# Two of a fused kernel's orders: an eviction moved from ScalarE to VectorE, and units 4 and 5 of the attention placed behind block 1's halves

## The chip, the cores and the metric

The kernel runs on 1 core of one Trainium2 chip. The metric is the device time of one execution in microseconds. TensorE (PE in the rows) multiplies matrices, VectorE (DVE) and ScalarE (ACT) do the elementwise work, GpSimd (POOL) a few small pieces, and SP issues the transfers. Each engine executes its own instructions strictly in program order and waits on semaphores where it needs another's result.

## The reference, cut to what matters

```python
# attention: B, H, S, D = 4, 8, 576, 64
scores = scale * np.matmul(q, k.transpose(0, 1, 3, 2))
scores = np.where(causal, -1e9, scores)
a = np.exp(scores - scores.max(-1, keepdims=True))
a /= a.sum(-1, keepdims=True) + 1e-09
local = np.matmul(a, v)
mem_out = (phi(q) @ M_prev) / (phi(q) @ z_prev + 1e-06)
attn = g * mem_out + (1 - g) * local
# feed-forward on x of shape (2304, 512), d_ff = 2048
h = x @ w_in
r = np.maximum(h, 0.0)
out = (r * r) @ w_out
```

All inputs and outputs are float32. Each token's 8 x 64 attention values are one row of x.

## The kernel before

**Attention units.** The list `order` holds 24 units, counted here from 0: one pair of heads of one batch entry with some of its four tiles of 128 queries. Units 0 to 3 are batch entry 0 with tiles 1 and 2 ("lo"), units 4 to 7 the same with tiles 3 and 4 ("hi"). A unit computes scores of a tile on TensorE into the PSUM tile `sp` (L583), VectorE evicts them with the mask and the row maximum into `e` (L604, `tensor_tensor_reduce`, two heads), ScalarE takes the exponential (L624), and the weights are transposed. In units 0 to 2 (`full`) that is done in float32 on TensorE: up to four transposed tiles in the PSUM tile `pxa`, evicted to `aF` (L643 to L646) by the engine that `PXE` names, its first letter for the first `pxa` of a tile of queries and its second for the second. Only tile 2 has a second one: two of 128x128. From unit 3 on the weights are split into two float16 halves `a`, by ScalarE (L662) and VectorE (L664), and SP transposes them by DMA to `aT` (L668). TensorE multiplies with the values into `acc` (L688), and VectorE adds to `feat`, the unit's features (L691). Unit i's buffers for k, q and v (`kd`, `qm`, `vv`) are loaded ahead as the unit two or three before gives them up.

**Blocks of tokens.** Four units of equal tiles make the features of 256 tokens, a block. Block 0 is the first 64 tokens of all four batch entries; block 1 is tiles 1 and 2 of batch entry 0, so units 0 to 3. `token_halves` (L706) makes a block's input: squares for a scale (L715), a high half on ScalarE (L722) and a low half on VectorE (L723), float16, for each of two tiles of tokens, and for each a transpose by DMA into `xT` (L724). `moe` then multiplies with the weights' halves: `up` (L989 to L991), relu and square on ScalarE, halves `gh` and `gl` (L1001, VectorE), and `oacc` (L960 to L962). Block 0 adds its groups of weights into `o` (L978).

**The order.** `ORD` merges the generators: units 0 to 3, then the weights' preparation, and block 0 beside them, then the other units with the blocks' matmuls behind. Within that, the framework's scheduler places each instruction on its engine by its own estimate of when it can start. `later(eng, x)` adds an edge to such an instruction that only orders: `x` is placed behind the instruction that `gate[eng]` holds, and no semaphore is waited for. Before the change such edges hold back weights (`put`) and the first unit (`lead`) behind block 0's tokens.

Of the kernel before, what the change touches and what calls it, by code (L numbers as in the profile page):

```python
# [14 lines left out]
AF = mybir.ActivationFunctionType  # L15
ALU = mybir.AluOpType
# [25 lines left out]
NEF = 3  # L42
NES = 6
PXT = 'av'
PXE = 'aa'
PHI = 1
ZW = D + 1
MW = 576
# [28 lines left out]

FIRST = 4
WA = 0
WE = 8  # L80
WE2 = 16
WH = 11
# [16 lines left out]
def fused_kernel(ctx: ExitStack, tc: tile.TileContext, t0_d, kk_d, qv_d, beta, w_in, w_out, out):  # L99
    nc = tc.nc  # L100
# [65 lines left out]
    gate = {}  # L166
# [286 lines left out]
    def attention(b, p, tiles, ld, after, early, sfull, full, ap, ap_early):  # L453
# [118 lines left out]
        def scores(group):  # L572
            sps = ps.tile([P, 2, 512], F32, tag="s", name="sp")
            c = 0
            at_col = []
            for i, ka, kb in group:
                qc = slice(QT[i][0] - D, sum(QT[i]) - D)
                cs = slice(c, c + kb - ka)
                at_col.append(cs)
                with tc.high_priority():  # L580
                    for x, (qt, kt) in enumerate(terms):
                        for h, hd in enumerate(heads):
                            mm = nc.tensor.matmul(  # L583
                                sps[:, h, cs], qt[hd, qc], kt[hd, ka:kb], start=x == 0, stop=x == len(terms) - 1
                            )
                            if x == h == 0 and lead:
                                later("t", mm)
                            if behind:
                                tc.add_manual_dep(mm.ins, behind.pop().ins.name, AFTER, reason="a batch comes late")
                            while parts:  # L590
                                tc.add_manual_dep(mm.ins, parts.pop().ins.name, WHOLE, reason="a batch starts whole")
                c = cs.stop
            for (i, ka, kb), cs in zip(group, at_col):
                q0 = QT[i][0]
                if ka == 0:
                    row[i] = (
                        ap.tile([P, 2, S], F32, tag="e", name="e", bufs=EB if ap is at else EB2),
                        at.tile([P, 2, 2], F32, tag="mx", name="mx", bufs=4),
                        at.tile([P, 2], F32, tag="sm", name="sm", bufs=4),
                    )  # L600
                e, mx, _ = row[i]
                s = int(ka > 0)
                for h in range(2):
                    nc.vector.tensor_tensor_reduce(  # L604
                        out=e[:, h, ka:kb],
                        in0=sps[:, h, cs],
                        in1=mask[:, 448 - q0 + ka : 448 - q0 + kb],
                        scale=-0.125,
                        scalar=3e38 if s == 0 else mx[:, h, 0:1],
                        op0=ALU.add,  # L610
                        op1=ALU.min,
                        accum_out=mx[:, h, s : s + 1],
                    )

        for i in [t for t in TORD if t in tiles]:
            q0, n = QT[i]
            ke = q0 + n
            for group in SGROUP[i]:
                scores(group)
            ns = 2 if any(ka for g in SGROUP[i] for t, ka, _ in g if t == i) else 1  # L620
            e, mx, sm = row.pop(i)
            for h in range(2):
                bs = mx[:n, h, ns - 1 : ns]
                ex = nc.scalar.activation(  # L624
                    e[:n, h, :ke], e[:n, h, :ke], AF.Exp, bias=bs, scale=-1.0, accum_out=sm[:n, h : h + 1]
                )
            behind[:] = [ex]
            u0, ur = e[:n, :, 0:D], e[:n, :, D:ke]
            if full:
                nb = 1 + i  # L630
                aT = at.tile([P, 8, P], F32, tag="aT16", name="aF")
                cols = [(0, D)] + [(D + c * P, P) for c in range(i)]
                for b0 in range(0, 2 * nb, 4):
                    bn = min(4, 2 * nb - b0)
                    px = ps.tile([P, 4, P], F32, tag=PXT, name="pxa", bufs=2)
                    for x in range(bn):
                        h, c = divmod(b0 + x, nb)
                        c0, cw = cols[c]
                        nc.tensor.transpose(px[:cw, x, :n], e[:n, h, c0 : c0 + cw], ident)
                    lo = [x for x in range(bn) if (b0 + x) % nb == 0]  # L640
                    for x0, xn, pn in [(x, 1, D) for x in lo] + runs([x for x in range(bn) if x not in lo]):
                        dst, src = aT[:pn, b0 + x0 : b0 + x0 + xn, :n], px[:pn, x0 : x0 + xn, :n]
                        if PXE[b0 // 4] == "a":  # L643
                            nc.scalar.copy(dst, src)
                        else:
                            nc.vector.tensor_copy(dst, src)  # L646
            else:
                nb = 1 + 2 * i
                tg = TAGS[i]
                if i < 3 and 3 - i in started:  # L650
                    a, aT, o = (*a12, 6 if i == 2 else 0)
                else:
                    a = ap.tile([P, tg * P], F16, tag=f"a{tg}", name="a")
                    aT = ap.tile([P, tg, P], F16, tag=f"aT{tg}", name="aT")
                    o = 6 if i == 2 else 0
                    if i < 3:
                        a12 = (a, aT)
                started.add(i)
                a, aT = a[:, o * P : (o + 2 * nb) * P], aT[:, o : o + 2 * nb]
                av = a[:n].rearrange("p (h x) -> p h x", h=2)  # L660
                for x, o0, w in ((u0, 0, D), (ur, P, i * P)):
                    nc.scalar.mul(av[:, :, o0 : o0 + w], x, SC)  # L662
                for x, o0, w in ((ur, P, i * P), (u0, 0, D)):
                    nc.vector.scalar_tensor_tensor(  # L664
                        out=av[:, :, o0 + w : o0 + 2 * w], in0=x, scalar=SC, in1=av[:, :, o0 : o0 + w],
                        op0=ALU.mult, op1=ALU.subtract,
                    )
                nc.sync.dma_start_transpose(out=aT[:, :, :n], in_=a[:n])  # L668
            nc.vector.scalar_tensor_tensor(
                out=sm[:n], in0=sm[:n], scalar=1e-9, in1=gm[:n, h0 : h0 + 2] if full else vz[:n],  # L670
                op0=ALU.add, op1=ALU.mult,
            )
            nc.vector.reciprocal(sm[:n], sm[:n])
            yield

            acc = ps.tile([P, 2, D], F32, tag="av", name="acc", bufs=2)
            for h in range(2):
                hd = slice(h * D, (h + 1) * D)
                if full:
                    mms = [(aT[: D if c == 0 else P, h * nb + c], v[: D if c == 0 else P, c, hd]) for c in range(nb)]  # L680
                else:
                    vh, vl = (vs[:, h, :, x * D : (x + 1) * D] for x in range(2))
                    mms = [(aT[:, h * nb], vh[:, 0]), (aT[:, h * nb], vl[:, 0])]
                    for c in range(1, i + 1):
                        hi, low = aT[:, h * nb + c], aT[:, h * nb + i + c]
                        mms += [(low, vh[:, c]), (hi, vh[:, c]), (hi, vl[:, c])]
                for x, (lhs, rhs) in enumerate(mms):
                    nc.tensor.matmul(acc[:n, h], lhs[:, :n], rhs, start=x == 0, stop=x == len(mms) - 1)  # L688
            for h in range(2):
                xo = memx[:n, i - 1, h]  # L690
                x = nc.vector.scalar_tensor_tensor(  # L691
                    out=xo, in0=acc[:n, h], scalar=sm[:n, h : h + 1], in1=xo, op0=ALU.mult, op1=ALU.add
                )
                step.setdefault(me, x)
            yield
# [10 lines left out]
    def token_halves(b, blk, xts, out_scale):  # L706
# [12 lines left out]
        nc.vector.reciprocal(sc, ss)  # L719
        for t, (src, hl, xt) in enumerate(zip(srcs, hls, xts)):  # L720
            hi, lo, s1 = hl[:, :DM], hl[:, DM:], sc[:, t : t + 1]
            nc.scalar.activation(hi, src, AF.Copy, scale=s1)  # L722
            nc.vector.scalar_tensor_tensor(out=lo, in0=src, scalar=s1, in1=hi, op0=ALU.mult, op1=ALU.subtract)  # L723
            nc.sync.dma_start_transpose(out=xt, in_=hl)  # L724
            nc.vector.tensor_scalar(
                out=out_scale[:, t : t + 1], in0=ss[:, t : t + 1], scalar1=ss[:, t : t + 1], scalar2=kmax[:, 0:1],
                op0=ALU.mult, op1=ALU.mult,
            )
# [429 lines left out]
```

## Time and profile before

| | before |
|---|---|
| median of 3 runs | 559.96 us (558.51 to 560.4) |
| the profiled execution | 559.57 us |
| its span in the trace | 557.8 us |
| busy: TensorE, VectorE, ScalarE, GpSimd | 93%, 81%, 74%, 3% of the span |
| mean granted TensorE clock | 0.977 |

The profiled execution's own time is 1.8 us over its span, and 0.39 us below the median of the runs. Shares of the span are means over stages with different limits, so the sections below read the trace by stretches of time.

### The profile page before, as it was taken

The page shows a single profiled execution, that of the slowest core. Times are in us where ns is not written, and L with a number is a line of the kernel's source. Part 1 is how long each engine was busy: PE and PEld are TensorE (multiplying, and loading weights), DVE is VectorE, ACT ScalarE, POOL GpSimd, SP SyncE. Part 2 cuts the span into 40 slices and gives each one's busy share as a digit, 9 for nine tenths or more (in the row PEclk, how much of TensorE's full clock was granted, in tenths as well). Part 3 has the DMA queues.
Part 4 walks back from the last instruction along what each step waited for, and adds up shares of the span by engine and source line. Part 5 has one row for each costly group of instructions (what it writes and reads, how often), then busy time and mean ns, then how long its engine had stood idle before and what let it go on. Part 6 is the DMA issues. An engine that isn't in the chain of part 4 may idle for free.

```text
span 557.8 us, 12617 instructions
## 1 busy us (share of the span) xinstructions
PE 520.5 (93%) x4767; PEld 368.6 (66%) x4767; DVE 452.4 (81%) x1425; ACT 412.4 (74%) x888; POOL 14.3 (3%) x20
## 2 busy tenths in 40 slices
PE   5656999988999999999989999999999999999996
PEld 4544766656777776667756777667766766447776
DVE  6898879998997989999977878888686788745645
ACT  3699997894798889989877777889666734566252
POOL 1000000111010000000000000000000000000000
PEclk9967999998999999999999999999999999999999
DMA  8968931488566858978657466481745320100002
GB/s 309 405 221 245 330 106 39 124 159 189 114 155 147 186 136 148 190 155 201 119 103 145 121 138 123 76 145 47 115 93 78 93 43 1 39 1 1 1 1 75
DMA packets 133132, 71.37 MB, mean 128 GB/s; under 512 B 115408, under 2 KB 121552, under 8 KB 133072
## 3 DMA queue, kind: packets, MB, share of 16 engines
q1 hardware_dynamic: 133072, 70.57, 53.9%
q8 instruction: 37, 0.61, 0.4%
q14 instruction: 23, 0.19, 0.1%
HBM read 37.53 MB, written 4.72 MB: 76 GB/s over the span
## 4 chain that ended last, share of the span: by engine, by line
PE 54%; DVE 22%; ACT 10%; DMA 10%; issue 2%; SPq 1%; POOL 0%; ACTq 0%; DVEq 0%
PE up L989 6%; PE up L990 5%; PE up L991 5%; PE seven L850 5%; DVE e L604 5%; PE oacc L962 5%; PE oacc L960 5%; PE oacc L961 5%; PE acc L688 4%; DVE a L664 4%; PE sp L583 3%; ACT e L624 3%; DMA xT<-hl 3%; PE seven L823 2%; PE seven L821 2%; PE seven L822 2%
## 5 line engine op out<-in xcount | busy, mean ns | idle before, releaser
L989 PE MATMUL up<-xT,w 128*128 128x256 f16 x448 | 123.8, 276 | 5.8 <-DMA xT<-hl 5.2
L991 PE MATMUL up<-xT,w 128*128 128x256 f16 x448 | 123.8, 276 | 0.0
L990 PE MATMUL up<-xT,w 128*128 128x256 f16 x448 | 123.8, 276 | 0.0
L624 ACT ACTIVATE e<-e,mx 128x320 f32<-128x320 f32 (+3 forms) x128 | 77.6, 609 | 40.5 <-DVE feat L691 22.4
L960 PE MATMUL oacc<-w,gh 128*128 128x512 f16 x224 | 84.9, 379 | 0.6 <-ACT gh L998 0.5
L961 PE MATMUL oacc<-w,gh 128*128 128x512 f16 x224 | 84.9, 379 | 0.0
L962 PE MATMUL oacc<-w,gl 128*128 128x512 f16 x224 | 81.3, 379 | 0.0
L664 DVE SCALAR_TENSOR_TENSOR a<-e,a 128x128 f16<-128x128 f32 x116 | 65.3, 573 | 10.7 <-ACT a L662 9.8
L662 ACT ACTIVATE a<-e 128x128 f16<-128x128 f32 x116 | 54.9, 522 | 2.2 <-DMA aT<-a 1.8
L989 PEld LDWEIGHTS <-w 128*128 128x128 f16 x448 | 44.4, 99 | 16.4 <-DMA xT<-hl 5.7
L990 PEld LDWEIGHTS <-w 128*128 128x128 f16 x448 | 44.4, 99 | 11.6 <-issue 1.2
L991 PEld LDWEIGHTS <-w 128*128 128x128 f16 x448 | 44.5, 99 | 8.5 <-issue 0.4
L995 ACT ACTIVATE r<-up,gam 128x512 f32<-128x512 f32 x48 | 32.4, 675 | 23.6 <-PE up L991 20.9
L604 DVE CUSTOM_DVE_ANT_0 e<-sp,mask 128x320 f32<-128x320 f32 (+3 forms) x128 | 47.1, 417 | 2.3 <-PE sp L583 2.3
L688 PE MATMUL acc<-vs,aT 128*128 128x64 f16 x1138 | 43.1, 193 | 4.8 <-DMA aT<-a 3.2
L688 PEld LDWEIGHTS <-aT 128*128 128x128 f16 x1138 | 39.3, 98 | 10.3 <-DMA aT<-a 4.3
L1001 DVE TENSOR_TENSOR gl<-r,gh 128x512 f16<-128x512 f32 x56 | 38.3, 684 | 5.8 <-ACT gh L998 5.3
L960 PEld LDWEIGHTS <-gh 128*128 128x128 f16 x224 | 21.9, 98 | 22.2 <-ACT gh L998 0.9
L962 PEld LDWEIGHTS <-gl 128*128 128x128 f16 x224 | 21.7, 98 | 22.1 <-DVE gl L1001 0.5
L850 PEld LDWEIGHTS <-g 128*128 128x128 f16 x336 | 32.9, 98 | 4.2
L996 ACT ACTIVATE r<-r 128x512 f32<-128x512 f32 x56 | 35.1, 627 | 0.6
L961 PEld LDWEIGHTS <-gh 128*128 128x128 f16 x224 | 21.9, 98 | 19.9
(192 smaller groups left out, 1033.7 us busy)
## 6 DMA issues: line engine op xcount, KB each, us to landing
raw<-in_w_in_dram SPq DMA_DIRECT2D x16, 512.0 KB, 6.6
raw<-in_w_out_dram SPq DMA_DIRECT2D x16, 512.0 KB, 7.5
vv<-in_qv_dram SPq DMA_DIRECT2D x16, 320.0 KB, 3.1
kd<-in_kk_dram SPq DMA_DIRECT2D x16, 288.0 KB, 3.1
out_dram<-o SPq DMA_DIRECT2D x12, 256.0 KB, 2.0
qm<-in_qv_dram SPq DMA_DIRECT2D x8, 321.0 KB, 2.9
qm<-in_qv_dram SPq DMA_DIRECT2D x8, 193.0 KB, 4.1
vv<-in_qv_dram SPq DMA_DIRECT2D x8, 192.0 KB, 3.2
```

The costliest lines, as they stand in the source:

```text
L604: nc.vector.tensor_tensor_reduce(out=e[:, h, ka:kb], in0=sps[:, h, cs], in1=mask[:, 448 - q0 + ka : 448 - q0 + kb], scale=-0.125, scalar=3 ...
L624: ex = nc.scalar.activation(e[:n, h, :ke], e[:n, h, :ke], AF.Exp, bias=bs, scale=-1.0, accum_out=sm[:n, h : h + 1])
L662: nc.scalar.mul(av[:, :, o0 : o0 + w], x, SC)
L664: nc.vector.scalar_tensor_tensor(out=av[:, :, o0 + w : o0 + 2 * w], in0=x, scalar=SC, in1=av[:, :, o0 : o0 + w], op0=ALU.mult, op1=ALU.sub ...
L688: nc.tensor.matmul(acc[:n, h], lhs[:, :n], rhs, start=x == 0, stop=x == len(mms) - 1)
L850: mms.append(nc.tensor.matmul(x[blk] if len(blks) == 1 else x[:, blk], g[j][:, i0, a, blk, p], t_side(j, p, m, i1), start=j == js[0] and p ...
L960: nc.tensor.matmul(acc[t], gh[:, u, ts], w_out_op(f, 0), start=f == f0, stop=False)
L961: nc.tensor.matmul(acc[t], gh[:, u, ts], w_out_op(f, 1), start=False, stop=False)
L962: nc.tensor.matmul(acc[t], gl[:, u, ts], w_out_op(f, 0), start=False, stop=f == f1)
L989: nc.tensor.matmul(uo, w_in_op(f, k, 0), x_op(k, 0), start=k == 0, stop=False)
L990: nc.tensor.matmul(uo, w_in_op(f, k, 0), x_op(k, 1), start=False, stop=False)
L991: nc.tensor.matmul(uo, w_in_op(f, k, 1), x_op(k, 0), start=False, stop=k == NK - 1)
```

## The change

`PXE` becomes 'ad': the second `pxa` of tile 2 in units 0, 1 and 2, one instruction of 128x256 each, is evicted by VectorE and no longer by ScalarE. And `token_halves` keeps block 1's last high half in `gate["bs"]` and its last low half in `gate["bv"]`; the exponentials of units 4 and 5 get an ordering edge to the first, their evictions an edge to the second.

```diff
-PXE = 'aa'
+PXE = 'ad'
...
+BEHIND = (4,5,)
...
-                    nc.vector.tensor_tensor_reduce(
+                    x = nc.vector.tensor_tensor_reduce(
                         out=e[:, h, ka:kb],
...
                         accum_out=mx[:, h, s : s + 1],
                     )
+                    if me in BEHIND:
+                        later("bv", x)
...
                     e[:n, h, :ke], e[:n, h, :ke], AF.Exp, bias=bs, scale=-1.0, accum_out=sm[:n, h : h + 1]
                 )
+                if me in BEHIND:
+                    later("bs", ex)
...
-            nc.scalar.activation(hi, src, AF.Copy, scale=s1)
-            nc.vector.scalar_tensor_tensor(out=lo, in0=src, scalar=s1, in1=hi, op0=ALU.mult, op1=ALU.subtract)
+            up = nc.scalar.activation(hi, src, AF.Copy, scale=s1)
+            low = nc.vector.scalar_tensor_tensor(out=lo, in0=src, scalar=s1, in1=hi, op0=ALU.mult, op1=ALU.subtract)
+            if (b, blk) == blocks[1]:
+                gate["bs"], gate["bv"] = up, low
```

The scheduler makes more of it than these lines tell. Line numbers of the changed kernel are up to 7 higher. On **VectorE**, around block 1's low halves, `hl_1362` and `hl_1364`, before (`e_1806` is unit 5, `sp_1847` its second score group, `gl_1546` block 0):

```order
L664 SCALAR_TENSOR_TENSOR a_1813<-e_1801,a_1813 128x2x384
...
L556 RECIPROCAL nm_1607<-nm_1607 128x4
L1001 TENSOR_TENSOR gl_1546<-r_1544,gh_1545 128x512
L604 ISA e_1806,mx_1807<-sp_1847,mask_84,mx_1807 128x512
L604 ISA mx_1807 128x1
...
L519 RECIPROCAL vy_1590<-vy_1590 128x1
L558 TENSOR_TENSOR feat_382<-pm_1604,nm_1607 128x2x2x64
L723 SCALAR_TENSOR_TENSOR hl_1362<-feat_382,sc_1361,hl_1362 128x512
L723 SCALAR_TENSOR_TENSOR hl_1364<-feat_382,sc_1361,hl_1364 128x512
```


And of the change, the same place (`e_1656` and `e_1661` are unit 4, evicted before the change some 80 rows ahead of this place):

```order
L724 RECIPROCAL sc_1361<-ss_1360 128x2
L732 TENSOR_SCALAR osc_1359<-ss_1360,kmax_79 128x1 x2
L728 SCALAR_TENSOR_TENSOR hl_1362<-feat_382,sc_1361,hl_1362 128x512
L985 SCALAR_TENSOR_TENSOR o_1042<-oacc_1457,kj_1515,o_1042 128x512
L728 SCALAR_TENSOR_TENSOR hl_1364<-feat_382,sc_1361,hl_1364 128x512
L605 ISA e_1656,mx_1657<-sp_1651,mask_84 128x448
L605 ISA mx_1657 128x1
...
L605 ISA e_1661,mx_1662<-sp_1651,mask_84 128x64
L605 ISA mx_1662 128x1
```


Block 1's lows stood behind all evictions of units 4 and 5 and behind three of their four `a`; now they stand ahead of the first of them.

On **TensorE**, the start of block 1 (`up_5165`), before; `acc_1677` is unit 4's tile 3, of 22 matmuls, and `oacc_1552` block 0's last group:

```order
L962 LDWEIGHTS gl_1546
L962 MATMUL oacc_1552<-w31_1346,gl_1546 128x512
L547 MATMUL pm_1637<-qm_1613,pe_1618 128x130 x2
L688 LDWEIGHTS aT_1669
L688 MATMUL acc_1677<-vs_1600,aT_1669 128x64
...
L989 LDWEIGHTS w0_463
L989 MATMUL up_5165<-xT_1358,w0_463 128x256
L990 LDWEIGHTS w0_463
L990 MATMUL up_5165<-xT_1358,w0_463 128x256
```


And of the change, where unit 4's second score group `sp_1702` has come to stand just ahead:

```order
L969 MATMUL oacc_1551<-w29_1340,gl_1498 128x512
L584 MATMUL sp_1702<-kd_980,qm_982 128x512 x2
L967 LDWEIGHTS gh_1497
L967 MATMUL oacc_1552<-w28_1337,gh_1497 128x512
...
L969 MATMUL oacc_1552<-w29_1340,gl_1498 128x512
L996 LDWEIGHTS w0_463
L996 MATMUL up_5165<-xT_1358,w0_463 128x256
L997 LDWEIGHTS w0_463
L997 MATMUL up_5165<-xT_1358,w0_463 128x256
```


Block 1's first 11 matmuls now stand ahead of the last twelve `oacc` matmuls of block 0, and 21 of its 24 first ones ahead of `acc_1677`. Unit 5's score groups `sp_1796` and `sp_1847`, ahead of block 1 before, are behind its 11th and 48th matmul.

On **SP**, the queue of transfers, before, from unit 8's load of k (`kd_1790`) on; `kd_1644` and `qm_1646` are unit 6's:

```order
L435 DMA kd_1790<-in_kk_dram 128x320
L439 DMA qm_1792<-in_qv_dram 128x386
L442 DMA vv_1794<-in_qv_dram 128x384
L435 DMA kd_1928<-in_kk_dram 128x320
L668 DMA_TRANSPOSE aT_1669<-a_1668 128x14x128
L668 DMA_TRANSPOSE aT_1710<-a_1709 128x18x128
L439 DMA qm_1646<-in_qv_dram 128x130
L439 DMA qm_1646<-in_qv_dram 128x256
L668 DMA_TRANSPOSE aT_1814<-a_1813 128x14x128
L435 DMA kd_1783<-in_kk_dram 128x576
L724 DMA_TRANSPOSE xT_1358<-hl_1362 128x8x128
L724 DMA_TRANSPOSE xT_1358<-hl_1364 128x8x128
```


And of the change:

```order
L436 DMA kd_1790<-in_kk_dram 128x320
L440 DMA qm_1792<-in_qv_dram 128x386
L443 DMA vv_1794<-in_qv_dram 128x384
L731 DMA_TRANSPOSE xT_1358<-hl_1362 128x8x128
L731 DMA_TRANSPOSE xT_1358<-hl_1364 128x8x128
L436 DMA kd_1644<-in_kk_dram 128x576
L440 DMA qm_1646<-in_qv_dram 128x130
L440 DMA qm_1646<-in_qv_dram 128x256
L673 DMA_TRANSPOSE aT_1669<-a_1668 128x14x128
```


The two transposes of block 1 have passed eight transfers, three transposes of units 4 and 5 among them. From the instruction at 208.92 us of the trace before (the second low half of unit 12) to the end, VectorE and ScalarE have the same order in both kernels, and TensorE and SP soon after.

## Rows read from the trace of the kernel before

**Rows 1.** Page, busy tenths in 40 slices of 13.9 us; PEclk: granted clock.

```profile
PE   5656999988999999999989999999999999999996
...
PEclk9967999998999999999999999999999999999999
```

**Rows 2.** By stretches: us; busy PE, PEld, DVE, ACT, POOL; clock, DMA share, GB/s.

```profile
102.70:124.60 21.90, 21.17 (x149) 12.37 (x147) 21.66 (x64) 19.48 (x41) 2.88 (x2) 1.00 0.85 169
124.60:140.00 15.40, 12.33 (x122) 9.40 (x123) 13.02 (x48) 8.00 (x19) 1.40 (x1) 0.89 0.79 186
128.80:133.20 4.40, 4.40 (x26) 3.31 (x27) 4.22 (x19) 0.83 (x1) 0.00 (x0) 0.61 0.90 253
140.00:203.85 63.85, 63.85 (x665) 47.49 (x662) 56.96 (x221) 54.80 (x135) 3.63 (x4) 1.00 0.70 153
203.85:278.40 74.55, 73.93 (x739) 52.84 (x740) 70.93 (x256) 65.17 (x143) 0.00 (x0) 1.00 0.80 158
```

**Rows 3.** TensorE's waits, 100 to 560 us: total, times, longest.

```profile
PE acc L688 <- DMA aT<-a: 3.2, 4, 1.7
PE up L989 <- DMA xT<-hl: 2.4, 1, 2.4
```

**Rows 4.** TensorE in order of time: start us, us, instruction, idle before.

```profile
117.07 1.13 PE L583 MATMUL sp<-kd,qm 64*128 64x512 f32 x4 [0.16 <-DVE mx L604]
...
125.09 0.19 PE L688 MATMUL acc<-vs,aT 128*128 128x64 f16 x1 [0.92 <-DVE vy L515]
125.46 0.91 PE L688 MATMUL acc<-vs,aT 128*128 128x64 f16 x21 [0.18 <-DVE vs L527]
128.78 0.28 PE L989 MATMUL up<-xT,w 128*128 128x256 f16 x1 [2.40 <-DMA xT<-hl]
```

**Rows 5.** Chain that ended last, 85 to 140 us: start, us, what.

```profile
102.70 3.11 DMA vv<-in_qv_dram
...
123.30 1.32 DVE hl L723 x2
...
130.27 0.21 PE up L990
...
133.46 0.11 PE up L991
```

**Rows 6.** VectorE: L604 and L664 in stretches; page, L1001's group.

```profile
98.90:124.60 25.70, 5.97 (x24) 1.00 0.73 145
...
102.60:124.60 22.00, 3.84 (x6) 1.00 0.84 168
...
L1001 DVE TENSOR_TENSOR gl<-r,gh 128x512 f16<-128x512 f32 x56 | 38.3, 684 | 5.8 <-ACT gh L998 5.3
```

**Rows 7.** DMA issues, 100 to 150 us: last figure is us to landing.

```profile
aT<-a SPq DMA_TRANSPOSE x8, 4.5
```

**Rows 8.** Chain that ended last, 140 to 204 us and 200 to 290; TensorE.

```profile
by line: PE up L989 12.8%; PE up L991 12.6%; PE up L990 12.6%; PE sp L583 12.0%; PE oacc L962 11.3%; PE oacc L961 11.1%; PE oacc L960 11.1%; PE acc L688 11.0%; PE pm L547 5.3%; PE vt L514 0.5%
...
203.85 0.64 PE pm L547 x4
...
208.92 0.96 DVE a L664
...
278.46 5.39 DMA aT<-a
...
283.89 0.99 PE L688 MATMUL acc<-vs,aT 128*128 128x64 f16 x28 [1.72 <-DMA aT<-a]
```

**Rows 9.** VectorE's waits, 100 to 280 us: total, times, longest.

```profile
DVE e L604 <- PE sp L583: 1.9, 3, 0.7
...
DVE vx L510 <- DMA vv<-in_qv_dram: 1.4, 3, 1.0
```

**Rows 10.** ScalarE in order of time.

```profile
72.71 0.42 ACT L644 COPY aF<-pxa 128x256 f32<-128x256 f32 x1
```

## The prediction

> **What bounds the kernel now.** The page first, its slices: TensorE's granted clock is under 9 tenths in the third and fourth slice, before 56 us, and then in one slice alone, 125 to 139 us; and from 56 us to the last slice TensorE is busy 9 tenths or more but for two slices, 112 to 139 us [rows 1]. So one place in the middle cost busy time and clock, and it is the one to look at. The view by stretches says who is full where [rows 2]: in 102.7 to 124.6 VectorE (21.66 of 21.90 us); in 124.6 to 140 nobody, at a mean clock of 0.89; in 140 to 203.85 TensorE, 63.85 of 63.85, with VectorE at 56.96; in 203.85 to 278.4 both nearly, VectorE with 70.93 of 74.55.
>
> TensorE's waits after 100 us are few [rows 3]: one of 2.4 us for xT, block 1's transposed tokens, and 3.2 us in four waits for aT, transposed softmax weights. Its instructions in order of time show two more just before the xT wait, both for unit 4's values [rows 4]: idle 0.92, 0.18 and 2.40 us, with 1.1 us of small products between. Right behind, the clock falls: the mean in 128.8 to 133.2 is 0.61 [rows 2], and a 256-column matmul takes 0.21 us in the chain, later 0.11 [rows 5]. The chain also shows why xT was late: a load of v at 102.70, then, but for gaps, VectorE alone until block 1's low halves (L723) at 123.30 and the transposes behind them.
>
> **The change part by part.**
>
> *Block 1 earlier.* VectorE's order shows what now stands behind block 1's second low half and stood ahead of it: the evictions of units 4 and 5 (L604), their a (L664, six instructions), one gl, one o, one feat and vy's small steps. The stretch up to 124.6 holds 5.97 us of L604 and 3.84 us of L664, all of it theirs; gl is 0.68, o of the same size counts the same [rows 6], and I put the small ones at 0.5, an estimate: 11.7 us. Rows on VectorE overlap a little (two low halves are 1.32 us in the chain, and 0.68 each would be 1.36), so I use 10.5. The lows ended at 124.6 and now end at 114.1. They also need unit 3's products, which don't move; behind those come squares, copies and lows one after another, so I take 114.5. TensorE had xT 4.2 us after the lows (124.6 to 128.78), hence now at 118.7. On SP's queue the two transposes pass eight transfers (three aT, three kd, two qm); unit 8's three loads stay ahead of them.
>
> *When TensorE asks.* It was through with everything ahead of block 1 at 126.37 (125.46 + 0.91 [rows 4]). Now stand behind block 1's first matmul: 12 oacc matmuls of 512 columns (twice 0.11 each, 2.6), two score groups (1.13 each), a pm group (0.64 [rows 8]) and unit 4's acc (0.91): 6.4 us, and the waits of 0.92 and 0.18 with them. It asks at 118.9, and xT is there within half a microsecond either way. So 3.50 us of idle time go, and with them the stretch at half clock: 4.4 x (1 - 0.61) = 1.7 us. **TensorE saves 5.2 us.**
>
> *What waits instead.* Unit 4's second score group needs the PSUM tile that VectorE frees behind block 1's lows: 114.5 + 1.5 (a quarter of the 5.97 us) = 116.0. TensorE gets there six oacc matmuls and one score group before it asks for xT, at 116.5. Unit 4's acc needs its aT: behind the lows VectorE has half of the evictions (3.0), gl, o and small ones (1.9) and a third of the 3.84, which is 120.7; a transpose lands 4.5 us later [rows 7], 125.2. TensorE has 21 matmuls of block 1 (2.3), the oacc (2.6), a score group (1.1) and half a pm in between: 118.9 + 6.3 = 125.2. That is a tie. Queued behind a late acc is the rest of block 1. I charge 0.5 us; bounds are 0 and 1.7, the longest wait for an aT now [rows 3].
>
> *VectorE as the next limit.* In 140 to 203.85 the chain runs over TensorE alone; from 208.92 on it is VectorE's and ScalarE's until a transpose at 278.46, and TensorE waits 1.72 us at its end [rows 8]. From 208.92 on the order on these two engines is what it was. So what counts is how much sooner VectorE gets there. Its work is the same; it can only save waits. Those on TensorE's scores (1.9) and on loads of v (1.4), which TensorE's reads set free, can go, 3.3 us, all before 209 [rows 9]. Its other waits are on ScalarE, which waits for VectorE in turn. Bounds of the gain: 0, and 5.2 - 0.5 = 4.7. I take **3.5**: the row says 3.3, and a little of ScalarE's lateness should go too. Behind 278 the order is unchanged and the shift is carried to the end.
>
> *The evictions.* Three copies of 128x256 go from ScalarE to VectorE. ScalarE takes 0.42 us [rows 10]; VectorE does 512 columns in 0.68 [rows 6], so 256 lie between 0.34 and 0.68, and I take 0.42. VectorE gets 1.3 us, ScalarE is relieved of as much, all before 100 us, under cover of TensorE's 9 tenths and more [rows 1]. The first of them stands behind block 0's lows, so block 0's xT does not move. I take 0; without the cover, 1.3 us either way.
>
> *Sum.* The profiled execution took 559.57 us (span 557.8), 0.39 below the median of 559.96. 559.57 - 3.5 = 556.1, against the median 556.5: **556.2 us**.
>
> **The rivals.**
>
> *All of the 5.2 us reaches the end: 554.4.* For it: ScalarE has room, 54.80 of 63.85 us [rows 2]. Against: the chain behind 208. Chance 0.15.
>
> *Nothing is won: 559.6, up to 560.9 with the copies.* VectorE is the bound from 102.7 on, TensorE comes early to the wait at 283.89 and stands there for 1.72 + 5.2 us. For it: VectorE's 99% and 95% [rows 2]. Against: its 6.9 us of idle in 140 to 203.85. With the case that the edges don't do what they say, since unit 3's products hold the halves up anyway: 0.2. The Trainium skill's Perfetto Trace Analysis, Identifying the Most-Contended Engine, speaks for this rival: occupancy is a fair measure for Vector and Scalar, matmul busy time is not one for TensorE, its weight-load share is. By that measure TensorE stands at 47.49 of 63.85 us, 74%, in 140 to 203.85, and VectorE at 89%; VectorE would be the bound there already, and the sum 0 instead of 3.5. The trace disagrees so far: the chain of that stretch is TensorE's [rows 8].
>
> *The wait moves to 283.89 and costs clock there.* With VectorE 3.5 us sooner TensorE stands 1.72 + 1.7 = 3.4 us, as long as the gaps before 128.78, and half clock behind it costs another 1.7, on the path: 557.9. For it: equal length. Against: those 1.72 us cost no clock. Chance 0.15.
>
> *Slower.* Units 4 and 5 come ten microseconds later on VectorE, and TensorE's queue is in order: where aT lands after TensorE has done what stands ahead, it waits, and block 1 with it. Two groups of acc each for units 4 and 5, each as late as the longest aT wait now, 1.7 us: 6.8, and one more stretch at half clock, 1.7, less the 5.2: 562.9. It decides at 0.9 us of lateness each with the clock, 1.3 without. For it: the tie at unit 4's acc. Against: 24 up matmuls stand ahead of the second one. Chance 0.12.
>
> **How the numbers follow.** Forecast (554.5 to 557.5) 0.38, full gain 0.15, clock 0.15, nothing won 0.2, slower 0.12. 0.3% (1.7 us) is about what a measurement of this kernel tells from no change. Faster by more than that: 0.38 + 0.15 + 0.15 = 0.68; same 0.2; slower 0.12. The range reaches from the full gain with the copies' 1.3 us to nothing won with the copies: 553.1 to 560.9. The forecast's own range is 554.5 to 557.5.
>
> **What would show it.** No wait for xT between 115 and 130 us, and the clock at 1.00 from 60 us to the last slice. Block 1's L723 over before 116 us. Unit 4's acc without a wait over 1 us. The instruction of VectorE at 208.92 some 3.5 us sooner, and the wait at 283.89 longer than 1.72 us. Wrong would be: over 2 us of L688 waits between 118 and 150, VectorE no sooner at 208.92, or xT still waited for.

## The result, and the profile after

The changed kernel took 565.55 us (median of 14 runs, 562.07 to 567.98) against 560.31 us (14 runs, 558.51 to 561.0) before: a ratio of 1.0087, 95% interval 1.007 to 1.0103. It is slower, by 5.2 us in the medians, where 3.8 us less was forecast; 565.55 lies outside the range. The profiled execution is the fastest of the 14 (562.07 us, span 560.3, mean clock 0.966 against 0.977), so its trace shows only 2.5 us of span to explain; a second profile, below, shows more. The profiles of three kernels of the experiments below are of their slowest execution (edges_only 562.57 us at a median of 560.26, edges_unit5 561.9 at 560.15, exp5_only 564.05 at 560.95), so a profile's end can lie 2 or 3 us off its kernel's median.

The page of the changed kernel, busy tenths and granted clock in 40 slices of 14.0 us, answers to [rows 1]:

```profile
PE   4656899998999999999989999999999999999996
PEclk9667899999899999999999999999999999999999
```

The slice at 125 to 139 us, which had 8 tenths, is mended in the clock. In its place the slices at 56 to 70 and 140 to 154 us show 8 tenths. TensorE in order of time (start us, us, instruction, in brackets the idle time before it and who ended it), against [rows 4, 8]:

```profile
64.61 0.71 PE L548 MATMUL pm<-qm,pe 128*128 128x130 f32 x4 [2.73 <-DVE feat L696]
...
121.33 0.27 PE L996 MATMUL up<-xT,w 128*128 128x256 f16 x1
...
139.18 0.47 PE L584 MATMUL sp<-kh,qh 64*128 64x448 f32 x2 [1.35 <-DVE mx L605]
...
141.74 1.36 PE L693 MATMUL acc<-vs,aT 128*128 128x64 f16 x22 [0.79 <-DMA aT<-a]
...
286.05 0.99 PE L693 MATMUL acc<-vs,aT 128*128 128x64 f16 x28 [2.48 <-DMA aT<-a]
```

Block 1's first matmul (121.33) waits for nothing, 7.5 us sooner than at 128.78. The 3.50 us of idle time there are gone. But 2.73 us stand at 64.61, 2.14 at 139 to 142, and at 286.05 the wait that was 1.72 us is 2.48. The stretches (columns as in [rows 2]) show half clock (0.50, which is 1.2 of 2.4 GHz) behind the first two, which costs up to half of each stretch, 1.7 us:

```profile
66.25:69.66 3.41, 3.41 (x20) 2.45 (x17) 2.62 (x8) 3.41 (x9) 0.00 (x0) 0.50 1.00 316
141.34:144.76 3.42, 3.02 (x27) 1.91 (x28) 3.42 (x11) 3.00 (x5) 0.00 (x0) 0.50 0.17 48
```

VectorE in order of time shows both sources, and block 1's lows (L728) at 115.00 and 116.37, over at 117.1 where 114.5 was forecast:

```profile
62.15 0.43 DVE L200 TENSOR_SCALAR raw<-raw 128x512 uint32<-128x512 uint32 x1 [2.42 <-DMA raw<-in_w_in_dram]
...
64.09 0.47 DVE L696 SCALAR_TENSOR_TENSOR feat<-acc,sm,feat 128x64 f32<-128x64 f32 x2
...
115.00 0.75 DVE L728 SCALAR_TENSOR_TENSOR hl<-feat,sc,hl 128x512 f16<-128x512 f32 x1 [0.50 <-ACT hl L727]
...
116.37 0.74 DVE L728 SCALAR_TENSOR_TENSOR hl<-feat,sc,hl 128x512 f16<-128x512 f32 x1
...
135.74 0.82 DVE L511 TENSOR_REDUCE vx<-vv 128x1 f32<-128x640 f32 x1 [2.14 <-DMA vv<-in_qv_dram]
...
180.75 0.74 DVE L728 SCALAR_TENSOR_TENSOR hl<-feat,sc,hl 128x512 f16<-128x512 f32 x1
```

At 62.15 a shift of a weight tile (L200) has stood 2.42 us for its load, and feat (64.09), for which TensorE waits, is queued behind it. At 135.74 the reduction of a v stood 2.14 us for a load, and unit 5's a is behind it. The chain that ended last goes the same way:

```profile
56.40 5.65 DMA raw<-in_w_in_dram
...
132.55 3.16 DMA vv<-in_qv_dram
...
137.72 3.98 DMA aT<-a
...
210.30 0.94 DVE a L669
```

The last row is the one that answers to 208.92 in [rows 8]: VectorE reaches it 1.4 us later, not 3.5 sooner.

**Where TensorE stands against before.** The table is worked out from TensorE's rows in order of time of each kernel: at a place where the same TensorE work lies behind it in both orders, its start there minus that in the profile of before. The columns are the places by before's times; the last is the span's end. A dash: no such place.

| us later than before, at | 63 | 66 | 75 | 104 | 165 | 209 | 280 | 287 | end |
|---|---|---|---|---|---|---|---|---|---|
| changed kernel | -1.6 | 3.0 | 2.3 | 2.9 | 1.1 | 1.1 | 1.4 | 2.1 | 2.5 |
| again (the same, 2nd profile) | -0.3 | 5.9 | 5.1 | 5.1 | 3.2 | 4.0 | 4.3 | 6.7 | 7.1 |
| before_again | -0.1 | 0.5 | 0.5 | 0.5 | 0.1 | 0.1 | 0.4 | 0.6 | 0.5 |
| copies_only | 0.4 | 0.7 | 3.9 | 3.6 | 4.2 | 5.9 | - | 9.4 | 18.9 |
| copies01_edges | 0.5 | 1.6 | 2.5 | 2.9 | 1.0 | 1.9 | 2.8 | 5.2 | 5.8 |
| copy0_exp4 | 0.1 | 0.5 | 2.2 | 2.4 | 1.3 | 1.7 | 1.7 | 4.2 | 4.1 |
| copy1_exp4 | 0.2 | 0.2 | 0.2 | 0.3 | -1.0 | -0.7 | -0.6 | 1.2 | 1.2 |
| copy12_edge5 | -1.5 | -1.2 | 1.2 | 1.4 | 2.8 | 3.8 | 3.9 | 6.4 | 6.3 |
| edges_only | 0.3 | 0.3 | 0.3 | 0.3 | -3.2 | 0.1 | - | - | 3.0 |
| edges_unit5 | -2.4 | 2.1 | 2.5 | 2.5 | -0.3 | 0.5 | - | - | 2.3 |
| exp5_only | 0.1 | 1.1 | 1.1 | 1.1 | -1.4 | 1.0 | - | 2.5 | 4.4 |
| exp4_only | 0.2 | 0.2 | 0.2 | 0.9 | 0.8 | 3.1 | - | 4.4 | 9.0 |
| shift_behind_fc | -0.1 | 0.1 | 4.6 | 5.0 | 5.6 | 7.3 | - | - | 8.6 |
| free_first | 1.1 | 2.6 | 6.6 | 6.8 | 8.7 | 12.6 | - | 13.0 | 17.5 |
| edges_less_vx | -0.2 | -0.2 | -0.2 | -0.5 | -3.6 | -2.4 | - | - | 1.8 |
| before_less_vx | -0.6 | 0.3 | 0.3 | 0.0 | - | 2.3 | - | 0.1 | 4.1 |
| before_raw8 | 0.0 | 0.1 | 3.8 | 3.9 | 8.2 | 8.9 | 9.1 | 11.7 | 12.0 |
| after_raw8 | -0.4 | 0.2 | 6.2 | - | 4.1 | - | - | - | 9.1 |

In its two profiles the changed kernel loses 2.9 and 5.1 us ahead of 104 us, gets back 1.8 and 1.1 by 209, and loses 0.7 and 2.4 around 284.

### The profile page after: what moved, and what is told of

It is laid out like the page before. It is cut to its first block, busy times and chain, and to the rows that moved or that the text cites. A ratio compares the mean times of both kernels' runs of the same rounds, so it can differ in the third digit from the quotient of the medians.

```text
span 560.3 us, 12621 instructions
## 1 busy us (share of the span) xinstructions
PE 521.5 (93%) x4767; PEld 369.3 (66%) x4767; DVE 452.8 (81%) x1428; ACT 411.6 (73%) x885; POOL 14.2 (3%) x20
## 4 chain that ended last, share of the span: by engine, by line
PE 43%; DVE 29%; DMA 12%; ACT 11%; issue 3%; SPq 1%; POOL 0%; ACTq 0%; DVEq 0%
DVE e L605 6%; PE seven L857 5%; DVE a L669 5%; PE oacc L969 4%; PE oacc L968 4%; PE oacc L967 4%; DMA aT<-a 4%; PE up L996 3%; PE acc L693 3%; PE up L997 3%; DMA raw<-in_w_out_dram 3%; ACT e L627 3%; PE up L998 3%; DMA raw<-in_w_in_dram 3%; PE seven L829 2%
## 5 line engine op out<-in xcount | busy, mean ns | idle before, releaser
L1008 DVE TENSOR_TENSOR gl<-r,gh 128x512 f16<-128x512 f32 x56 | 40.1, 717 | 5.2 <-ACT gh L1005 4.7
```

## The experiments

**Theory A** after the result: the loss is made before 75 us, by the orders that the copies bring. **Theory B**: it is made behind block 1, by late aT. First the two parts apart, the changed kernel again, and unit 5's edges alone:

```diff
copies_only:  -BEHIND = (4,5,)   +BEHIND = ()
edges_only:   -PXE = 'ad'        +PXE = 'aa'
edges_unit5:  -PXE = 'ad'        +PXE = 'aa'
              -BEHIND = (4,5,)   +BEHIND = (5,)
```

> The changed kernel itself once more, for a second profile. Theory A (the time is lost before 100 us: VectorE stands still for weight loads that were issued later, TensorE then waits for feat and its clock falls): its times spread over 562 to 568 us again, and the stretch up to 105 us is 2 us or more longer than before's, more so in a slower execution. Theory B (it is lost in 130 to 145 us, to late aT and the clock there): up to 105 us it stands within 1 us of before, and block 1 comes out of 130 to 160 us some 3 us late.

> The three copies on VectorE, no edges; up to about 108 us the engines' orders are those of the changed kernel. Theory A: slower than before by as much as the changed kernel or more, 563 to 570 us, with the wait of TensorE for feat near 64 us and a stretch at half clock behind it. Theory B: the copies are hidden, within 0.3% of before, 558.5 to 561.5 us.

> The edges without the copies; up to about 108 us the orders are those of before. Theory A: block 1's lows end near 114 us, and 1 to 3.5 us of it reach the end: 556.5 to 559 us, with a spread as small as before's. Theory B: the late aT eats the gain and more, 562 to 566 us.

> Edges for unit 5 alone, no copies: unit 4's evictions stay ahead of block 1's lows, so the lows end some 5 us sooner than before instead of 8 to 10. Theory A: half of the gain of the edges alone, 558 to 560 us. Theory B: the later aT are those of unit 5 and 4 together, so about half of the loss, 560 to 563 us.

Measured: again 567.15 us (4 runs, 566.66 to 568.85); copies_only 577.62 us, ratio 1.0309 [1.027, 1.0348]; edges_only 560.26 us, 0.9992 [0.9977, 1.0008]; edges_unit5 560.15 us, 0.9999 [0.9984, 1.0014]. So the copies lose, and the edges win nothing: edges_only came out between its two theories (559 us at most, 562 at least). The second profile of the changed kernel (span 564.9) has more of all that the first had. TensorE, VectorE, and the stretch behind, in its rows:

```profile
66.84 1.23 PE L548 MATMUL pm<-qm,pe 128*128 128x130 f32 x4 [3.63 <-DVE feat L696]
...
288.92 0.99 PE L693 MATMUL acc<-vs,aT 128*128 128x64 f16 x28 [2.45 <-DMA aT<-a]
```

```profile
64.38 0.43 DVE L200 TENSOR_SCALAR raw<-raw 128x512 uint32<-128x512 uint32 x1 [3.03 <-DMA raw<-in_w_in_dram]
```

```profile
63.50:70.30 6.80, 3.46 (x14) 2.40 (x15) 5.02 (x20) 6.70 (x15) 0.00 (x0) 0.59 0.68 214
288.80:292.20 3.40, 3.28 (x35) 1.76 (x36) 2.08 (x13) 2.33 (x6) 0.00 (x0) 0.68 0.46 102
```

A wait of 3.03 us for the load, 3.63 us for feat, half clock for twice as long, and half clock also behind the aT wait at 288.92. copies_only has the changed kernel's order up to about 108 us, but not the wait for feat near 64 us that Theory A named: its profile loses 3.2 us between 66 and 75, with a wait of 1.19 us for win_e, a weight maximum, at 71.14 and half clock from 72 to 79 us. And it is worse than the change by 12 us though it has less in it: its order differs from before's through to the end, while the change's order rejoins that of before near 209 us. Two edits of a few rows each thus change the rows far behind them, and their times do not add up.

Then kernels that differ in which unit's copy is moved, all with late orders of before (and with fewer edges than the change); and one edge more on the changed kernel:

```diff
copy0_exp4, copy1_exp4, copy12_edge5, copies01_edges (moved copies: unit 0; 1; 1 and 2; 0 and 1):
-                        if PXE[b0 // 4] == "a":
+                        if PXE[b0 // 4] == "a" or me not in PXU:
copy0_exp4, copy1_exp4:  edges only for unit 4's exps; copy12_edge5: BEHIND = (5,);
copies01_edges: BEHIND = (4,)
shift_behind_fc (in to_float, tile 24 behind the step of tile 21):
+            later(f"fc{LEAD.get(n)}", x)
```

> Only the first full unit's copy on VectorE, and the order-only edge for unit 4's exps alone (ScalarE). From about 75 us on every engine's order is that of its pair, copy1_exp4, and late it is that of before. Theory A (the copy of the first unit reorders VectorE: a step that waits for a weight load stands ahead of feat and of the steps that free the raw buffers, so loads go out later, TensorE waits for feat and its clock falls): the early loss is there, TensorE stands 2 to 4 us for feat near 64 us, and the time is 3 to 7 us above that of copy1_exp4. Theory B (a copy costs VectorE its own 0.42 us or nothing): within 1 us of copy1_exp4.

> Only the second full unit's copy on VectorE, the same edge; the first unit's copy stays on ScalarE and up to about 70 us the orders are those of before. Theory A: no wait for feat near 64 us, up to 75 us within 0.7 us of before; the whole 556 to 560 us, with before's small spread. Theory B: as copy0_exp4.

> The copies of the second and third full unit on VectorE, edges for unit 5 alone; early order that of before up to about 70 us, late order that of before. Theory A: no early loss, 556 to 560 us. Theory B: two copies, up to 0.8 us on before, and whatever the edges give.

> The changed kernel with the third full unit's copy back on ScalarE: two copies, 0.42 us of VectorE less. Its transfers are issued in the changed kernel's order and its late order is that of before. Theory A (it is the order that the first two copies bring): as slow as the changed kernel, 563 to 567 us, half clock in 60 to 75 us. Theory B (each copy has its share): a third of the loss gone, 561.5 to 564 us.

> The kernel before once more, for a second profile. Theory A (the early loss belongs to the orders with copies on VectorE): no stretch at half clock between 60 and 75 us, the matmul group of 92.4 us within 1 us of there. Theory B (the early loss comes and goes with any order): a stretch at half clock in 60 to 75 us, and that group 2 us or more later.

> The changed kernel with one more order-only edge: the shift of weight tile 24, which waits for its load, stands behind the step of tile 21 that frees a raw buffer, and so behind feat. The three copies and the eviction ahead of the freeing step of tile 17 stay. The order from about 110 us on is another one, so only the stretch up to 105 us is read. Theory A: the wait for feat near 64 us is under 0.5 us instead of 2.7 to 3.6, and the first matmul of the group that began at 65.3 us before and at 67.3 to 70.9 in the changed kernel begins by 66.3. Theory B: it begins as late as in the changed kernel.

Measured: copy0_exp4 563.73 us, 1.0058 [1.0038, 1.0079]; copy1_exp4 561.58 us, 1.0019 [1.0001, 1.0036]; copy12_edge5 566.42 us, 1.0085 [1.0057, 1.0113]; copies01_edges 565.0 us, 1.0089 [1.0064, 1.0115]; before_again 560.14 us; shift_behind_fc 568.98 us, 1.0143.

copy0_exp4 and copy1_exp4 have one copy each and the same order from 75 us on. They stand 2.0 us apart at 75 us in the table and 2.15 us in the medians: not the copy's 0.42 us but where it stands costs. before_again is within 0.7 us of before at every place of the table. But edges_unit5, whose order up to 108 us is before's, lost 4.5 us at 64 in its profiled execution: TensorE came 2.4 us sooner, waited 1.74 us for feat, and ran at half clock from 62 to 69 us. So before's early order can have such a loss too. At 75 us the ten profiles without unit 0's copy that keep before's buffers stand at -0.2 to 1.2 us but for this one at 2.5; the five with it at 2.2 to 5.1. The mechanism that I had named, a wait for feat, holds only in part. copy0_exp4 has no wait for feat; it waits 1.23 us for win_e at 71 us. In shift_behind_fc the wait for feat is gone, as Theory A said, and TensorE waits at 72 us instead, with half clock behind it:

```profile
72.29 0.29 PE L215 MATMUL gr<-identb,win_e 128*128 128x128 bf16 x1 [1.78 <-DVE win_e L237]
```

Without the third copy (copies01_edges, which also lacks unit 5's edges) the time is 565.0 us, as Theory A had it, though at full clock (1.00) from 60 to 75 us; what the third copy costs by itself was not run. And copy12_edge5 was a miss by 6 us: it loses 2.4 us between 66 and 75 though the first unit's copy stays where it was, 2.4 between 104 and 209, and 2.5 around 284.

**Do the buffers of the weight loads make it?** One more raw buffer, and the steps that free buffers put ahead again:

```diff
before_raw8, after_raw8:
-NRAW = 7
-NFC = 12
+NRAW = 8
+NFC = 10
free_first: evictions of unit 1's first group behind the freeing step of tile 17,
            w of tile 12 and the shift of tile 24 behind that of tile 20
+            tc.add_manual_dep(x.ins, step.ins.name, AFTER, reason="buffers come free first")
```

> The kernel before with eight raw buffers for weight loads instead of seven, and ten fc buffers instead of twelve to make room. From about 110 us its late order is that of before. Theory A (which buffer comes free when decides the loads, and TensorE follows them before 100 us): its loads go out up to 2 us sooner, and the time is 557 to 560 us. Theory B (it is VectorE's and ScalarE's work that decides, and fewer fc buffers hold it up): 560 to 564 us.

> The changed kernel with eight raw buffers and ten fc buffers. Its late order is another one, so the stretch up to 105 us is read. Theory A: with one buffer in reserve a freeing step that VectorE does late holds up no load; TensorE has no wait for feat over 0.5 us near 64 us and no stretch at half clock in 60 to 75 us, and is at 104 us within 1 us of before_raw8. Theory B: it loses 3 to 5 us against before_raw8 there, as the changed kernel did against before.

> The changed kernel with order-only edges on VectorE that put the step which frees a raw buffer (tile 17) back ahead of the first eviction behind it, and that of tile 20 ahead of the shift of tile 24, which waits for its load; the three copies stay. Only the stretch up to 105 us is read, since the late order is another one. Theory A (the loads go out later because those steps come later): the shift of tile 24 waits under 1 us for its load instead of 2.4 to 3.0, TensorE's wait for feat near 64 us is under 1 us, and at 104 us TensorE is within 1.2 us of before. Theory B (VectorE's own time): 2.5 us or more behind before at 104 us, as the changed kernel.

Measured: before_raw8 572.44 us, 1.0221 [1.0179, 1.0263]; after_raw8 568.61 us, 1.0156; free_first 577.28 us, 1.0303. Both theories missed the pair: both kernels wait early for win_e, before_raw8 2.92 and after_raw8 4.91 us; the extra raw buffer and the two fc buffers less were not run apart, so which of them makes it is not shown. free_first took away the wait of tile 24's shift and that for feat, and still lost 5.5 us by 75: tile 27's shift then waited 2.92 us for its load, and TensorE for feat and win_e in four waits (1.31, 0.23, 1.18, 1.82). Whichever step was put ahead, another that TensorE needs came late.

Neither kernel puts the loads themselves back, though, and SP's issues show that the copies move two of them. SP in before_again, then in the changed kernel (the loads of weight tiles 24 to 27, L272 and L273):

```profile
55.88 2.96 SPq L272 DMA_DIRECT2D raw<-in_w_in_dram  x4
```

```profile
56.40 1.53 SPq L273 DMA_DIRECT2D raw<-in_w_in_dram  x3
...
64.20 0.33 SPq L273 DMA_DIRECT2D raw<-in_w_in_dram  x1
```

Before, the four go out together. In the changed order the step that frees a buffer for tile 27 (the `fc` step of tile 20) has come to stand on VectorE behind the shift of tile 24, which waits for its own load, so tile 27's load goes out last and late. win_e is the maximum over tiles 24 to 27 (`weight_scale`), and TensorE waits for it. The chain of copies_only goes that way, through the moved copy `aF` too:

```profile
63.33 3.77 DMA raw<-in_w_in_dram
...
67.89 2.40 DVE fc L203 x4
...
70.29 0.33 DVE aF L651
...
70.89 0.20 DVE win_e L232
```

The profiles fall into two groups. Tile 27's load goes out at 56.9 to 58.5 us in the ten without unit 0's copy, at 63.1 to 66.4 in the five with it, and at 62.6 and 63.8 in shift_behind_fc and free_first. These two therefore do not speak against the late loads as the cause; a kernel with the copies and both loads in their old places was not run.

**Does VectorE eat the edges' gain?** The reduction for v's scale takes fewer columns, so its result is another; this frees VectorE of about 0.5 us for each narrow unit. Here Theory A is that VectorE sets how soon block 2 is ready, Theory B that TensorE's queue does:

```diff
before_less_vx (on before), edges_less_vx (on edges_only):
-            nc.vector.tensor_reduce(out=vx, in_=vc, axis=AX.XY, ...
+            nc.vector.tensor_reduce(out=vx, in_=vc[:, :1], axis=AX.XY, ...
exp4_only, exp5_only: no copies, the edge for the exps of unit 4 (5) alone
```

> The kernel before, with the largest absolute value of v taken over the first 128 of up to 640 columns only (so part of the reduction is left out): some 0.5 us less on VectorE for each narrow unit, 6 us between 100 and 209 us. Theory A (VectorE sets how soon block 2 is ready): block 1's lows end 1 to 2 us sooner, and 1 to 4 us reach the end: 556 to 559 us. Theory B (TensorE's queue sets it): within 1 us of before.

> The edges without the copies, and the same shorter reduction. Theory A (the edges' lead on TensorE, 7 us at block 1's first matmul, is given up because VectorE brings block 2's low halves no sooner): with 6 us less on VectorE block 2's lows end at 174 to 177 us instead of 180.9, block 2 starts 3 us or more before 188, and the whole comes to 554 to 557.5 us, 1 us or more under the shorter reduction alone. Theory B: block 2 starts within 1 us of 188 and the time is that of the edges alone, 559 to 561.5 us.

> No copies; the order-only edge for unit 4's exps on ScalarE alone, none on VectorE. Early order that of before, late order another one in part. Theory A (edges alone win nothing at the end, since VectorE brings block 2 no sooner): 558.5 to 562 us, block 2's low halves begin within 1.5 us of 179. Theory B (it was the edges on VectorE that made units 4 and 5 late): block 2's lows 2 us sooner, 556 to 558.5 us.

> No copies; the edge for unit 5's exps alone. Theory A: 558.5 to 562 us. Theory B: 556 to 558.5 us.

Measured: before_less_vx 563.69 us, 1.0071 [1.0045, 1.0097]; edges_less_vx 562.7 us, 1.004 [1.0022, 1.0058]; exp4_only 566.81 us, 1.0107 [1.0076, 1.0138]; exp5_only 560.95 us, 1.0026 [1.0006, 1.0046]. exp5_only's total is in Theory A's range; the other three missed both theories, and each of these orders is another one late. The stretch up to block 2 goes with Theory A in part. VectorE in order of time, block 1's and block 2's lows of edges_only, then block 2's of edges_less_vx:

```profile
114.12 0.75 DVE L728 SCALAR_TENSOR_TENSOR hl<-feat,sc,hl 128x512 f16<-128x512 f32 x1 [0.50 <-ACT hl L727]
...
180.93 1.41 DVE L728 SCALAR_TENSOR_TENSOR hl<-feat,sc,hl 128x512 f16<-128x512 f32 x2
```

```profile
177.09 0.74 DVE L728 SCALAR_TENSOR_TENSOR hl<-feat,sc,hl 128x512 f16<-128x512 f32 x1
```

In edges_only block 1's lows are 9.2 us sooner than before's 123.30 [rows 5], and block 2's, 66 us later, begin at 180.93 (the expectation calls that their end), where before_again has 179.25. By the table TensorE's lead is 3.2 us at 165 and nothing at 209. With VectorE relieved (edges_less_vx) 3.6 us become 2.4. That is for Theory A; but before_less_vx, relieved as much, stands 2.3 us late at 209, so an order of its own moves as much as what was sought, and VectorE's part is made likely, not shown. VectorE's stretch from a weight maximum near 93.6 us to block 2's lows, in before_again and edges_only:

```profile
93.70:179.20 85.50, 82.05 (x765) 58.06 (x763) 78.15 (x275) 69.60 (x163) 8.67 (x8) 0.98 0.66 139
```

```profile
93.50:180.90 87.40, 85.00 (x804) 60.21 (x803) 78.62 (x277) 71.70 (x167) 9.64 (x8) 1.00 0.62 135
```

VectorE is idle for 7.35 us (85.50 - 78.15) in the one and for 8.78 us in the other: TensorE's lead has not taken its waits away. Later edges_only leads by 2.3 us again (at 306 us), and it is 3.0 us behind at 429, in this slowest of its executions: a wait for aT, and half clock behind it:

```profile
422.91 1.67 PE L693 MATMUL acc<-vs,aT 128*128 128x64 f16 x50 [1.87 <-DMA aT<-a]
```

```profile
425.00:430.00 5.00, 5.00 (x28) 2.99 (x25) 0.96 (x5) 2.59 (x7) 0.00 (x0) 0.72 0.00 0
```

None of these kernels is faster than the kernel before: edges_unit5 and edges_only are as fast.

## Why the prediction was wrong

**Block 1 earlier: right.** The lows were forecast to end at 114.5 and ended at 117.1, with an o between them; the first matmul was forecast for 118.9 and came at 121.33, in an order that starts 2.9 us late. There was no wait for xT, and the clock was 1.00 from 116 to 139 us. But this was not the one place to look at: [rows 1] has a third slice of 8 tenths, 279 to 293 us, which the prediction passed over, and the wait in it grew.

**The evictions: the step that failed.** "I take 0; without the cover, 1.3 us either way" counted three copies by their duration. The order that they bring cost 2.9 us at 104 us in the profiled execution and 5.1 in the second. What they moved was not counted: the prediction speaks of the order from 100 us on alone. Ahead of it the copies put an eviction of unit 1 before a step (L202, now L203) that frees a raw buffer. VectorE's order, before and now:

```
L202 SCALAR_TENSOR_TENSOR fc_736<-raw_578 128x512
L202 SCALAR_TENSOR_TENSOR fc_829<-raw_584 128x512
L604 ISA e_798,mx_799<-sp_793,mask_84 128x320
...
L203 SCALAR_TENSOR_TENSOR fc_736<-raw_578 128x512
L605 ISA e_798,mx_799<-sp_793,mask_84 128x320
...
L203 SCALAR_TENSOR_TENSOR fc_829<-raw_584 128x512
```

That step frees the buffer for tile 24's load. The chain, VectorE and TensorE of before_again have the same load, its shift and the products behind feat without the copies:

```profile
55.88 4.43 DMA raw<-in_w_in_dram
```

```profile
60.40 0.52 DVE L199 TENSOR_SCALAR raw<-raw 128x512 uint32<-128x512 uint32 x1 [0.60 <-DMA raw<-in_w_in_dram]
```

```profile
63.62 0.71 PE L547 MATMUL pm<-qm,pe 128*128 128x130 f32 x4 [0.36 <-DVE feat L691]
```

The load went out at 56.40 instead of 55.88 and took 5.65 us instead of 4.43, so the shift ran at 62.15 instead of 60.40; why the load took longer is not shown. TensorE's nine tenths were no cover, since its next product stood behind that shift on VectorE. Not all of the 2.73 us is the copies': those products came 1.0 us later than in before_again (64.61 against 63.62), and TensorE asked for them 1.4 us sooner (61.88 against 63.26). With up to 1.7 us for the half clock that makes some 2.7 us of loss, an estimate from these rows, against 2.4 in the table (2.9 less 0.5). Tile 27's load, 5.7 us later than in before_again, is the other path, and the one on which copies_only and copy0_exp4 lost: it stands in their chains, with win_e behind it. In the chains of copy1_exp4 and edges_only no weight load stands between 60 and 76 us. That these two loads are the whole cause is not shown, since no run put both back.

**VectorE as the next limit: mis-sized.** Of 5.2 us, 3.5 were to reach 208.92, made of 3.3 us of VectorE's waits. From 104 to 209 us TensorE won 1.8 and 1.1 us in the changed kernel's two profiles, 1.0 in copy1_exp4, 0.7 in copy0_exp4 and 0.2 in edges_only. Of the two kinds of wait that were to go, those for scores went and those for loads of v grew; VectorE's waits in the changed kernel, 100 to 280 us, against [rows 9]:

```profile
DVE vx L511 <- DMA vv<-in_qv_dram: 4.4, 3, 2.1
...
DVE e L605 <- PE sp L584: 0.3, 1, 0.3
```

Scores fell from 1.9 to 0.3 us, loads of v rose from 1.4 to 4.4, and to 3.4 in edges_only. The rival that nothing is won was the nearer one for this stretch, and its mechanism fits: block 2's lows come no sooner, whatever TensorE's lead. The rule of the Trainium skill that stood beside it (Perfetto Trace Analysis, Identifying the Most-Contended Engine), that busy matmul time says little of TensorE and VectorE's share is a fair measure, agrees with that, and the chain of before, which ran over TensorE from 140 us, misled me.

**The wait at 283.89: the place and the price were a rival's, the reason was not.** It was to grow because TensorE comes sooner. TensorE came later (1.4 and 4.3 us at 280), and aT later still: the wait is 2.48 and 2.45 us. The clock fell behind it, as that rival had it, in five of the six profiles of changed orders that rejoin before's late order. copy1_exp4 was 0.6 us ahead at 280 and is 1.2 behind at 287. Its rows, TensorE and the stretch:

```profile
283.39 1.11 PE L695 MATMUL acc<-vs,aT 128*128 128x64 f16 x28 [1.78 <-DMA aT<-a]
```

```profile
283.00:286.40 3.40, 3.01 (x33) 1.65 (x34) 2.34 (x13) 1.41 (x4) 0.00 (x0) 0.66 0.75 143
```

**The slower rival** named the side; its place gave up to 3.8 us. TensorE waited 1.35 us (unit 6's score group, for an eviction of unit 5) and 0.79 us (unit 5's aT), with the half clock from 141.34 behind it (up to 1.7 us more). In edges_only the waits there were 0.93 and 1.09 us, for the second aT of units 4 and 5, at full clock, and the time stayed where it was.

**What stays open:** whether the two late loads make up all of the 3 to 5 us ahead of 75 us, and why the changed kernel's runs spread over 5.9 us where before's 14 beside them spread over 2.5 (23 later runs of before: 4.2). The two profiles say only that the early wait and the clock behind it vary most (4.6 us and 6.2 us lost from 63 to 66).

## What to carry to other kernels

Where a scheduler sets the order, an edit's price is that of the order that it brings, from its first row to the last: compare the whole order, ahead of the place meant too, and look for steps that free a load's buffer and steps that wait for a load, with something that TensorE needs behind them. When a test edit takes away one wait and another comes, look whether it put the loads back at all, before giving up the cause. A lead on the engine that waits is worth what the engine that feeds it can follow with; measure that at the next hand-over (here block 2's lows), not at the first.

## What the runs showed of the hardware that was not expected

Waits of like length do and do not cost TensorE's clock. At the aT wait near 284 us, 1.72 us (before), 2.02 (before_again) and 2.48 (changed kernel) were followed by no half clock; 1.78 us (copy1_exp4) and 2.45 us (again) were, at means of 0.66 and 0.68 in the stretches shown above, and so were 2.45, 2.54 and 2.75 us (copies01_edges, copy0_exp4, copy12_edge5).

VectorE can be held up by GpSimd. In the changed kernel two gl took 2.47 us at 139.99, where the page's mean is 0.717 for one, and GpSimd's kl ran from 139.91 for 1.41 us; at 124.46 a two-column sm took 1.17 us, beside a kl from 124.11 for 1.49 us. The Trainium skill's GPSIMD Engine Reference (Specifications) has it that the two share SBUF interfaces and contend when VectorE reads two SBUF inputs; gl, with two, agrees.

It goes by who starts first. In the nineteen profiles together, the 17 gl that began 0.07 to 0.59 us after a kl took 0.82 to 1.91 us; the 30 that began up to 0.64 us before a kl, or within 0.02 us of it, took 0.68 to 0.69.
